# A transformer block on one core: W1, W2 and Wo copied inside DRAM into blocks with long runs, and loaded from the copies

## The chip, the core and the metric

The kernel runs on one core of a Trainium2 chip. Five engines work side by side, each through its own list of instructions: PE (matrix products; PEld is its weight load), ACT (exponentials and other functions), DVE (elementwise work), POOL (small work here) and SP, which here only issues DMAs. Semaphores tie them together. Sixteen DMA engines move data between DRAM and the on-chip memory SBUF, which has 128 partitions. Matrix products end in PSUM, eight banks of 128 x 512 fp32 values.

The metric is the device time of one execution in microseconds (us). The kernel before takes 1090.35 us (median of 3 runs, 1087.95 to 1093.55).

## What is computed

One pre-norm transformer layer on 2048 rows of width 1024, bf16, with 32 heads of width 32 and a feed-forward part of width 3584. `b1` and `b2` are the biases of the feed-forward part; `B_x` is not used.

```python
x = A_x
h = x + softmax_attention(layernorm(x) @ wqkv) @ wo      # 32 heads, no mask
h2 = h + gelu_tanh(layernorm(h) @ w1 + b1) @ w2 + b2
```

## The kernel before

**How the order comes about.** The program does not write its instruction lists by hand. `Graph.add` records tasks (a matmul group, an exponential, a DMA) with an estimated duration and the buffers that they read and write; `Graph.schedule` (L109) then simulates the engines with these estimates and fixes the order of every engine's list. `assign` gives each task the semaphore waits that the order does not already imply. For a DMA the planner charges an issue time, bytes divided by one fixed rate, and one fixed latency; it does not look at the length of a run. DMAs are issued by SP alone, in the planned order, over 24 "lanes" (semaphores); a DMA that has to wait holds up all that stand behind it on SP.

**Phases.** The 2048 rows are handled in eight units of 256 rows (`u` or `qb` = 0 to 7), and heads in eight groups `g` of four.

- Lead-in: x is loaded and normalized, transposed (`xnT`), and Q, K and V of group 0 are projected; the first exponentials start.
- First phase: for each further group, K and V are projected for all rows and Q for the rows needed soon, while attention runs for the row blocks 0 and 1 (and 2 for groups 1 and 2, `EXTRA`). In this phase the SBUF that later holds the feed-forward weights still holds `wqkv` (the tiles `Wall`) and `xnT`.
- Then come `late_q` (the Q of the remaining row blocks, from the normalized x that was parked in DRAM as `x_scratch`, loaded into `xq`), and for each unit `wo(u)` (output projection and first residual), `ln2(u)`, `ffn1(u)` (W1, bias, GELU) and `ffn2(u, j)` (W2 in two halves of 512 columns), all as background work beside the attention of later row blocks.
- The tail: after the last exponential, `wo`, `ffn1` and `ffn2` of unit 7 (and the second half of `ffn2` of unit 6) run alone.

**Attention round.** Each round issues eight score matmuls (L784), two exponentials of 128 x 1024 (L795), eight matmuls with V (L821) and a sum of the exponentials by pairs on DVE (L836) that is added up by matmuls with ones (L850). ACT is given score matmuls first (`pick_pe`): they have priority over all other work of PE. Background products go out either as one full 128-column matmul (L549, and L552 where they are planned so from the start) or as four narrow ones of 32 columns (L546), depending on what stands beside them.

**Weights.** W1 (1024 x 3584), W2 (3584 x 1024) and Wo (1024 x 1024) are read anew for every unit. `wblock` loads 256 columns of W1, Wo or `wqkv` into one of four ring slots `R.w1` (trace name a_w1r), 512 KB: partition p gets eight rows of 512 bytes. `ffn2` loads 512 rows x 512 columns of W2 into one of seven slots `R.w2` (a_w2r), 512 KB: four rows of 1 KB per partition. `wo` takes all four slots of `R.w1`, two for each half of the output columns. The tail has a second set of rings (b_w1r with 14 slots, b_w2r with 7) in the memory that K and V leave free. In the trace the inputs w1 and w2 both appear as in_B_w_dram.

Of the kernel before, what the change touches and what calls it, by code (L numbers as in the profile page):

```python
# [12 lines left out]
P = 128  # L13
BF = dt.bfloat16
# [314 lines left out]
def build_kernel(nc, A_x, A_wqkv, A_wo, B_w1, B_b1, B_w2, B_b2, out):  # L329
    _, S, D = A_x.shape  # L330
# [6 lines left out]
    DC = D // P  # L337
    FC = F // P
# [8 lines left out]
    gr = Graph(N_LANES)  # L347
# [18 lines left out]
    def sb(area, name, shape, dtype, split=1, parts=1):  # L366


        off, n = area.take(shape, dtype)
        h = nc.alloc_sbuf_tensor_at(name, shape, dtype, offset=off)  # L370
        step = n // split
        bufs = []
        for i in range(split):
            ps = [gr.buf("SB", off + i * step, off + (i + 1) * step, (name, i)) for _ in range(parts)]
            bufs.append(ps if parts > 1 else ps[0])
        return h, (bufs if split > 1 else bufs[0])
# [33 lines left out]
    OT, B_OT_ = sb(top, "OT", [P, 3, G, 256], BF, 3 * G, 2)  # L410
# [12 lines left out]
    for k in range(6):  # L423
        h, b = sb(k_hi if k == 2 else ph0, "Wall%d" % k, [P, DC, 512], BF, 1, 4)
# [57 lines left out]
            return i  # L482

    R1 = Rings((ffn, 4), (ffn, 7), ffn, 2)
    lq, B_lq = sb(xq_lo, "lq", [P, 2, 512], BF, 2)
    assert xq_lo.cur <= hn_lo
    att_area = Area(att_lo)
# [11 lines left out]
    qd = nc.dram_tensor("q_scratch", [G, NCH, P, 512], BF, kind="Internal").ap()  # L499
    xd = nc.dram_tensor("x_scratch", [3, P, DC, 512], BF, kind="Internal").ap()  # L500
    B_xd = [gr.buf() for _ in range(3)]
    B_qd = [[gr.buf() for _ in range(NCH)] for _ in range(G)]


# [13 lines left out]
    def slot(nrel=1):  # L518
        return Slot(gr.buf(), nrel, (6, 7))
# [374 lines left out]
            job.pv(r, s)  # L894


    def wblock(R, src_ap, prio=1):
        s = R.next("w1", R.nw1)
        dma(R.w1[:, s, :, :], src_ap.rearrange("(dc p) c -> p dc c", p=P), P * DC * 512, writes=[R.B_w1[s]], prio=prio)
        return s  # L900

    def wo(u, tail=False):
        R = R1
        nb = 0
        R.cnt["w1"] += -R.cnt["w1"] % 4
        ws = [wblock(R, A_wo[:, 256 * k:256 * k + 256]) for k in range(4)]
        assert ws == [0, 1, 2, 3]
        for t in range(2):
            hs = 2 * (u % 2) + t
            tt = 2 * u + t  # L910
            dma(hch[:, hs, :], x2[tt * P:(tt + 1) * P, :], P * 2048, writes=B_hch[hs], prio=1)
            for j in range(2):
                s = ws[2 * j]
                c = slice(512 * j, 512 * j + 512)
                bank = nb if tail else slot()
                nb += 1
                order = range(G) if tail else [7, 0, 1, 2, 3, 4, 5, 6]
                for k, g in enumerate(order):
                    mm(bank, OT[:, u % 3, g, t * P:(t + 1) * P], R.w1[:, s:s + 2, g, :], k == 0, k == 7 and not tail,
                       [B_OT[u % 3][g][t], R.B_w1[s], R.B_w1[s + 1]], not tail)  # L920
                if tail:
                    mm(bank, ident[:, :], hch[:, hs, c], False, True, [B_ident, B_hch[hs][j]], False)
                    act(lambda a, hs=hs, c=c, bank=bank: a.activation(hch[:, hs, c], psum[:, bank, :], ACT.Copy), 512,
                        reads=[bb(bank)], writes=[B_hch[hs][j]], prio=-1)
                else:
                    drop(dve(lambda v, hs=hs, c=c, bank=bank: v.tensor_tensor(
                        hch[:, hs, c], psum[:, bi(bank), :], hch[:, hs, c], ALU.add),
                        c_dve_ps(512), reads=[bb(bank), B_hch[hs][j]], writes=[B_hch[hs][j]]), bank)
# [14 lines left out]
    def ffn1(u, tail=False):  # L943
        R = R2 if tail else R1
        for blk in range(FC // 2):
            s = wblock(R, B_w1[:, 256 * blk:256 * blk + 256])
            bank = blk % 6 if tail else slot()
            for f in range(2):
                for dc in range(DC):
                    mm(bank, R.w1[:, s, dc, f * P:(f + 1) * P], hnT[:, dc, :], dc == 0, dc == DC - 1,  # L950
                       [R.B_w1[s]] + B_hnT, not tail, (256 * f, 256 * f + 256))
            evict1(u, 2 * blk, bank, tail)
            if not tail and blk % 2:
                gelu(u, blk // 2)
# [32 lines left out]
    def ffn2(u, j, wide=False, W=None, banks=None):  # L987
# [3 lines left out]
        ws = []  # L991
        for q in range(FC // 4):
            s = W.next("w2", W.nw2)
            dma(W.w2[:, s, :, :], B_w2[512 * q:512 * q + 512, c].rearrange("(f p) c -> p f c", p=P),
                P * 4096, writes=[W.B_w2[s]], prio=1)
            ws.append(s)
        for t in range(2):
            bank = banks[t] if banks and banks[t] is not None else slot()
# [113 lines left out]
        attention_drain()  # L1112

    EXTRA = [1, 2]
    for g in range(1, G):
        rest_of_projections(g)
        if g == 2:
            proj(0, 0, 1, slot(), "dve")
        attention(0, [g])
        attention(1, [g])  # L1120
        if g in EXTRA:
            attention(2, [g])
    for g in range(1, 2):
        if g not in EXTRA:
            proj(0, g, 1, slot(), "dve")
    late_q(1, 1, [g for g in range(2, G) if g not in EXTRA])
    wo(0)
    ln2(0)
# [149 lines left out]
```

## Time and profile before

| | |
|---|---|
| median of 3 runs | 1090.35 us |
| the profiled execution | 1091.97 us, of which its span (first to last instruction) 1090.2 us |
| busy: PE, ACT, DVE | 96%, 93%, 69% of the span |
| idle of ACT from 76 to 1021 us | 8.4 us |
| last exponential ends | about 1021.9 us |
| DMA packets | 280146, of which 274976 under 2 KB; 178.03 MB |
| W1 loads (98 and, for the tail, 14) | 512 KB each, median 4.4 and 6.1 us from issue to landing |
| W2 loads (105 and 7) | 512 KB each, 5.7 and 6.6 us |
| Wo loads (32) | 512 KB each, 4.2 us |

How to read the views that follow. The *page* gives busy time and a strip of 40 equal slices of the span, each digit the busy share in tenths. A row of the *windows* view is `from:to length, PE busy (x instructions) PEld ... POOL busy, granted clock of PE, DMA share, GB/s`; the DMA share is the mean busy share of 16 DMA engines, and since it is put together from packets it can come out a little over 1. A row of the *timeline* is `start, length, engine, line, operation, out<-in, count [idle before <- what ended it]`. A row of *groups* ends in `xcount: shortest/median/longest ns, first and last start in us`. "issue" as a releaser means that the engine waited for nothing that the profile shows. SPq is SP's queue, where the length of a row is the issue of the DMA alone, not its transfer.

### The profile page before, as it was taken

What the parts mean: (1) busy time and instruction counts of PE and PEld (TensorE: products, weight loads), DVE (VectorE), ACT (ScalarE), POOL (GpSimd) and SP (SyncE); (2) the same over time, 40 slices, a digit from 0 to 9 for tenths busy, and PEclk for the clock granted to TensorE, in tenths of its full rate; (3) what the DMA queues carried; (4) which work ended last, traced back from release to release, by engine and by line L of the source; (5) the groups of instructions that cost most, each with busy time, mean ns of one, the idle gap of its engine ahead of it and who ended that gap; (6) DMA issues with size and microseconds to landing.
All of it is one profiled execution on the core that took longest, in us unless ns stands there. A gap on an engine that the chain in (4) does not pass through costs nothing.

```text
span 1090.2 us, 41817 instructions
## 1 busy us (share of the span) xinstructions
PE 1045.6 (96%) x19048; PEld 609.6 (56%) x19107; DVE 755.9 (69%) x1453; ACT 1014.5 (93%) x1116; POOL 43.4 (4%) x110
## 2 busy tenths in 40 slices
PE   8989999998899999999999999999999999999998
PEld 6656555554344664574475457446545754474483
DVE  7886666666576896599489659948974967696401
ACT  4989999999999999999999999999999999999650
POOL 3200000000010001001000100100010000000100
PEclk9999999999999999999999999999999999899999
DMA  7640010008464667665685766567586656987370
GB/s 194 199 123 11 14 41 3 2 3 287 142 167 133 183 180 209 210 189 154 209 251 157 220 215 189 155 217 233 142 239 205 182 179 160 308 236 228 96 246 20
DMA packets 280146, 178.03 MB, mean 163 GB/s; under 512 B 42656, under 2 KB 274976, under 8 KB 279200
## 3 DMA queue, kind: packets, MB, share of 16 engines
q1 hardware_dynamic: 279968, 175.35, 54.1%
q8 instruction: 150, 2.46, 0.9%
q14 instruction: 28, 0.23, 0.1%
HBM read 161.16 MB, written 10.49 MB: 157 GB/s over the span
## 4 chain that ended last, share of the span: by engine, by line
PE 54%; ACT 39%; DVE 5%; issue 1%; DMA 1%; SPq 0%; POOL 0%; POOLq 0%; DVEq 0%
ACT PT L795 35%; PE ps L549 18%; PE ps L546 12%; PE ps L784 8%; PE ps L821 6%; PE ps L552 5%; PE ps L850 3%; ACT PX L795 2%; DVE PS L836 2%; ACT uu L983 2%; DMA xrb<-in_A_x_dram 0%; DVE OD L866 0%; PE ps L1025 0%; SPq L570 0%; DVE OD L873 0%
## 5 line engine op out<-in xcount | busy, mean ns | idle before, releaser
L795 ACT ACTIVATE PT<-ps 128x1024 bf16<-128x1024 f32 x992 | 922.4, 1082 | 14.7 <-PE ps L784 14.3
L836 DVE TENSOR_TENSOR PS<-PT 128x1024 bf16<-128x1024 bf16 x434 | 286.6, 685 | 128.9 <-PE ps L850 68.1
L784 PE MATMUL ps<-QT,KT 32*128 32x256 bf16 x4096 | 205.3, 274 | 10.7 <-ACT PT L795 5.4
L821 PE MATMUL ps<-PT,V 128*32 128x256 bf16 x3968 | 174.4, 274 | 2.8 <-ACT PT L795 2.8
L784 PEld LDWEIGHTS ps<-QT,KT 32*128 32x128 bf16 x4096 | 61.2, 92 | 166.3 <-ACT PT L795 134.8
L850 PE MATMUL ps<-PS,ones 128*32 128x256 bf16 x1792 | 124.6, 275 | 4.8 <-DVE PS L836 4.0
L821 PEld LDWEIGHTS ps<-PT,V 128*32 128x32 bf16 x3968 | 102.1, 97 | 29.4 <-issue 6.8
L549 PE MATMUL ps<-hnT,a_w1r 128*128 128x256 bf16 x949 | 116.5, 274 | 1.1 <-DVE gT L961 0.5
L549 PEld LDWEIGHTS ps<-hnT,a_w1r 128*128 128x128 bf16 x949 | 87.9, 98 | 25.8 <-issue 14.5
L546 PE MATMUL ps<-a_w2r,gT 128*32 128x512 bf16 x1372 | 98.3, 381 | 0.4 <-DVE hch L1007 0.2
L549 PE MATMUL ps<-a_w2r,gT 128*128 128x512 bf16 x382 | 93.8, 380 | 4.2 <-issue 2.9
L546 PE MATMUL ps<-hnT,a_w1r 128*32 128x256 bf16 x2476 | 88.9, 274 | 4.0 <-issue 1.6
L961 DVE TENSOR_TENSOR gT<-ps,b1f 128x512 bf16<-128x512 f32 x98 | 67.2, 686 | 17.5 <-PE ps L546 9.3
L546 PEld LDWEIGHTS ps<-hnT,a_w1r 128*32 128x32 bf16 x2476 | 60.4, 96 | 20.6 <-issue 16.8
L1007 DVE SCALAR_TENSOR_TENSOR hch<-ps,hch 128x512 bf16<-128x512 f32 x32 | 21.9, 685 | 69.9 <-PE ps L552 47.1
L850 PEld LDWEIGHTS ps<-PS,ones 128*32 128x32 bf16 x1792 | 47.0, 96 | 30.7 <-DVE PS L836 14.2
L549 PEld LDWEIGHTS ps<-a_w2r,gT 128*128 128x128 bf16 x413 | 35.2, 98 | 47.4 <-issue 13.4
L549 PE MATMUL ps<-xnT,Wall 128*128 128x512 bf16 (+1 forms) x256 | 53.5, 344 | 4.5 <-DVE rr L876 2.8
L983 ACT ACTIVATE uu<-uu 128x1024 bf16<-128x1024 bf16 x49 | 53.9, 1108 | 0.0
L546 PEld LDWEIGHTS ps<-a_w2r,gT 128*32 128x32 bf16 x1372 | 30.0, 96 | 25.6 <-issue 14.0
L603 POOL CAST mvb<-mv 128x2 bf16<-128x2 f32 (+1 forms) x25 | 4.9, 201 | 987.2 <-DVE mv L600 987.2
L549 PE MATMUL ps<-Wall,xnT 128*128 128x128 bf16 (+1 forms) x443 | 43.9, 247 | 0.0
(89 smaller groups left out, 1007.9 us busy)
## 6 DMA issues: line engine op xcount, KB each, us to landing
a_w2r<-in_B_w_dram SPq DMA_DIRECT2D x105, 512.0 KB, 5.7
a_w1r<-in_B_w_dram SPq DMA_DIRECT2D x98, 512.0 KB, 4.4
a_w1r<-in_A_wo_dram SPq DMA_DIRECT2D x32, 512.0 KB, 4.2
b_w1r<-in_B_w_dram SPq DMA_DIRECT2D x14, 512.0 KB, 6.1
a_w1r<-in_A_wqkv_dram SPq DMA_DIRECT2D x11, 512.0 KB, 5.0
Wall<-in_A_wqkv_dram SPq DMA_DIRECT2D x17, 256.0 KB, 4.7
xrb<-in_A_x_dram SPq DMA_DIRECT2D x16, 256.0 KB, 4.0
hch<-in_A_x_dram SPq DMA_DIRECT2D x16, 256.0 KB, 5.2
```

The costliest lines, as they stand in the source:

```text
L546: fns.append(lambda p, j=j: p.matmul(psum[32 * j:32 * j + 32, bi(bank), c0:c1], lhsT[:, 32 * j:32 * j + 32], rhs, start=start, stop=stop, ...
L549: t.whole = lambda p: p.matmul(psum[:, bi(bank), c0:c1], lhsT, rhs, start=start, stop=stop, skip_group_check=True)
L552: t = pe(lambda p: p.matmul(psum[:, bi(bank), c0:c1], lhsT, rhs, start=start, stop=stop), occ, reads=reads, writes=[bb(bank)], mode="full" ...
L603: pool(lambda g: g.tensor_copy(mvb[:, sl, :], mv_l[:, sl, :]), 0.25, reads=B_mv[sl], writes=B_mvb[sl], prio=prio)
L784: return p.matmul(psum[:, 2 * us[h // 2] + h % 2, 256 * i:256 * i + 256], KT[32 * h:32 * h + 32, g, k0:k0 + P], QT[32 * h:32 * h + 32, qs, :],
L795: act(lambda a, u=u, k=k: a.activation(PTs[s][:, k, :, :], psum[:, 2 * u:2 * u + 2, :], ACT.Exp, bias=0.0, scale=SCALE), 1024, reads=[B_ps ...
L821: fns.append(lambda p, i=i, h=h: p.matmul(psum[32 * h:32 * h + 32, bi(bank), 0:256], V[:, g, 2 * r + i, 32 * h:32 * h + 32], PTs[s][:, h / ...
L836: dve(lambda v: v.tensor_tensor(PS[:, n, :, :], pairs[:, :, 0:256], pairs[:, :, 256:512], ALU.add), c_dve(1024, 2), reads=B_PTs[s], writes ...
L850: fns.append(lambda p, h=h, rhs=rhs, i=i: p.matmul(psum[32 * h:32 * h + 32, bi(bank), 256:512], ones32[:, :], rhs, start=False, stop=last, ...
L961: t = dve(lambda v: v.tensor_tensor(g[:, fc:fc + 2, :], psum[:, bi(bank), :].rearrange("p (f c) -> p f c", f=2), b1f[:, fc:fc + 2].unsquee ...
L983: act(lambda a: a.activation(w, w, ACT.Tanh, bias=0.0, scale=KT2), 1024, reads=[B_uu[i]], writes=[B_uu[i]], prio=-1)
L1007: drop(dve(lambda v, hs=hs, bank=bank, half=half: v.scalar_tensor_tensor(hch[:, hs, c], psum[:, bi(bank), :], half, hch[:, hs, c], ALU.mul ...
```

## The change

At the end of the first phase's recording, `block_copies` adds 30 DMAs from DRAM to DRAM: Wo in two blocks of 512 columns (1 MB each), W1 in 14 blocks of 256 columns and W2 in 14 blocks of 512 rows x 512 columns (512 KB each). Each block is laid out as SBUF wants it, so that a partition's part is one run: 8 KB for Wo, 4 KB for W1 and W2. The copies read their source in the same rows of 512 bytes or 1 KB as the loads did. Copy number i waits for exponential number `COPY0 + COPY_STEP * i` (96, 101, ... 241, counted from 0), has priority 3 and is issued by SP like every other DMA. All later loads of W1, W2 and Wo, the tail's too, read the copies and depend on them. Loads of `wqkv` for `late_q` stay as they were.

Wo is now loaded in two DMAs of 1 MB in place of four of 512 KB; the tiles `wov` lie over slots 0, 1 and 2, 3 of the ring `R.w1`, and the products of `wo` read them there. All products and sizes stay the same, and so do the planner's costs.

```diff
@@ -482,6 +482,7 @@
     R1 = Rings((ffn, 4), (ffn, 7), ffn, 2)
+    wov = [nc.alloc_sbuf_tensor_at("wov%d" % j, [P, DC, 512], BF, offset=R1.B_w1[2 * j].lo) for j in range(2)]
@@ -499,6 +500,12 @@
     B_xd = [gr.buf() for _ in range(3)]
+    w1d = nc.dram_tensor("w1_blocks", [FC // 2, P, DC, 256], BF, kind="Internal").ap()
+    w2d = nc.dram_tensor("w2_blocks", [2, FC // 4, P, 4, 512], BF, kind="Internal").ap()
+    wod = nc.dram_tensor("wo_blocks", [2, P, DC, 512], BF, kind="Internal").ap()
+    B_w1d = [gr.buf() for _ in range(FC // 2)]
+    B_w2d = [[gr.buf() for _ in range(FC // 4)] for _ in range(2)]
+    B_wod = [gr.buf() for _ in range(2)]
@@ -894,8 +901,26 @@
-    def wblock(R, src_ap, prio=1):
+    def block_copies():
+
+        jobs = []
+        for j in range(2):
+            jobs.append((wod[j], A_wo[:, 512 * j:512 * j + 512].rearrange("(dc p) c -> p dc c", p=P), P * DC * 1024, B_wod[j]))
+        for k in range(FC // 2):
+            jobs.append((w1d[k], B_w1[:, 256 * k:256 * k + 256].rearrange("(dc p) c -> p dc c", p=P), P * DC * 512, B_w1d[k]))
+        for j in range(2):
+            for q in range(FC // 4):
+                jobs.append((w2d[j, q], B_w2[512 * q:512 * q + 512, 512 * j:512 * j + 512].rearrange("(f p) c -> p f c", p=P),
+                             P * 4096, B_w2d[j][q]))
+        exps = [t for t in gr.tasks if t.kind == "exp"]
+        for i, (o_ap, i_ap, n, b) in enumerate(jobs):
+            dma(o_ap, i_ap, n, writes=[b], prio=3, after=[exps[COPY0 + COPY_STEP * i]])
+
+    def wblock(R, src_ap, prio=1, block=None):
         s = R.next("w1", R.nw1)
+        if block is not None:
+            dma(R.w1[:, s, :, :], w1d[block], P * DC * 512, reads=[B_w1d[block]], writes=[R.B_w1[s]], prio=prio)
+            return s
         dma(R.w1[:, s, :, :], src_ap.rearrange("(dc p) c -> p dc c", p=P), P * DC * 512, writes=[R.B_w1[s]], prio=prio)
         return s
@@ -903,20 +928,21 @@
         R.cnt["w1"] += -R.cnt["w1"] % 4
-        ws = [wblock(R, A_wo[:, 256 * k:256 * k + 256]) for k in range(4)]
-        assert ws == [0, 1, 2, 3]
+        for j in range(2):
+            dma(wov[j][:, :, :], wod[j], P * DC * 1024, reads=[B_wod[j]], writes=R.B_w1[2 * j:2 * j + 2], prio=1)
+        R.cnt["w1"] += 4
...
-                s = ws[2 * j]
+                s = 2 * j
...
-                    mm(bank, OT[:, u % 3, g, t * P:(t + 1) * P], R.w1[:, s:s + 2, g, :], k == 0, k == 7 and not tail,
+                    mm(bank, OT[:, u % 3, g, t * P:(t + 1) * P], wov[j][:, g, :], k == 0, k == 7 and not tail,
@@ -943,7 +969,7 @@
-            s = wblock(R, B_w1[:, 256 * blk:256 * blk + 256])
+            s = wblock(R, None, block=blk)
@@ -991,8 +1017,7 @@
-            dma(W.w2[:, s, :, :], B_w2[512 * q:512 * q + 512, c].rearrange("(f p) c -> p f c", p=P),
-                P * 4096, writes=[W.B_w2[s]], prio=1)
+            dma(W.w2[:, s, :, :], w2d[j, q], P * 4096, reads=[B_w2d[j][q]], writes=[W.B_w2[s]], prio=1)
@@ -1112,6 +1137,7 @@
     EXTRA = [1, 2]
+    COPY0, COPY_STEP = 96, 5
@@ -1123,6 +1149,7 @@
+    block_copies()
     late_q(1, 1, [g for g in range(2, G) if g not in EXTRA])
```

## The prediction

> **What bounds the kernel now.** I read the page's parts on busy time, slices and the chain first, then busy time by stage, then the tiles that the change loads.
>
> ```profile
> span 1090.2 us, 41817 instructions
> PE 1045.6 (96%) x19048; PEld 609.6 (56%) x19107; DVE 755.9 (69%) x1453; ACT 1014.5 (93%) x1116; POOL 43.4 (4%) x110
> DMA  7640010008464667665685766567586656987370
> ...
> q1 hardware_dynamic: 279968, 175.35, 54.1%
> PE 54%; ACT 39%; DVE 5%; issue 1%; DMA 1%; SPq 0%; POOL 0%; POOLq 0%; DVEq 0%
> ```
>
> ```profile
> core 0: us, PE busy (x) PEld busy (x) DVE busy (x) ACT busy (x) POOL busy (x), PEclk, DMA share, GB/s
> 76.00:273.00 197.00, 191.45 (x3941) 113.25 (x3952) 122.55 (x223) 196.26 (x214) 0.00 (x0) 1.00 0.18 57
> 273.00:293.00 20.00, 18.22 (x257) 7.66 (x256) 9.99 (x19) 18.34 (x20) 0.00 (x0) 0.92 0.42 128
> 293.00:1021.00 728.00, 704.63 (x13435) 403.56 (x13470) 547.12 (x1050) 721.97 (x785) 22.23 (x56) 0.99 0.67 196
> 1021.00:1090.00 69.00, 65.51 (x431) 40.03 (x434) 10.76 (x22) 20.23 (x37) 3.45 (x8) 0.98 0.38 124
> ```
>
> From 76 to 1021 us ACT never stops for long: it is idle 197 - 196.26 = 0.7 us, then 1.7 us, then 728 - 721.97 = 6.0 us, 8.4 us in all. Behind 1021 us only PE matters, 65.5 of 69 us busy. So the end is set by ACT's row of exponentials and then by a tail of matmuls; the chain gives DMA 1%. The queues are loaded (0.67 of the 16 engines), but what counts is whether somebody waits for a load:
>
> ```profile
> its engine sat idle before it (us, times) until:
>   issue: 30.3, 146
> ...
>   DMA QT<-q_scratch: 0.2, 1
> ```
>
> That is the view of the W2 ring's tile a_w2r. Its matmuls sat idle 0.2 us for any transfer at all, and for a small Q block; the same view of a_w1r (W1 and Wo) lists no DMA. In this trace all loads of the three weights are hidden. That leaves a change of these loads no more than the 8.4 us above, and of it only what DMA causes.
>
> **Part 1, the loads in long runs.** Rates come from stages in which one packet size prevails (512 B for W1, 1 KB for W2, 8 KB for the Q input xq), as GB/s over DMA share:
>
> ```profile
> 370.00:390.00 20.00, 19.64 (x413) 14.56 (x406) 19.63 (x39) 20.00 (x23) 0.00 (x0) 1.00 0.63 183
> 515.00:532.00 17.00, 16.62 (x280) 7.66 (x275) 10.04 (x21) 17.00 (x19) 0.00 (x0) 1.00 0.84 257
> 262.00:266.00 4.00, 3.22 (x69) 1.39 (x70) 3.23 (x9) 4.00 (x5) 0.00 (x0) 1.00 1.02 431
> ```
>
> 183/0.63 = 290, 257/0.84 = 306 and 431/1.02 = 423 GB/s. A block of 524 KB takes the queue 1.81, 1.71 or 1.24 us. For 4 KB I take 400, near the upper row: 1.31 us. So some 0.45 us are saved on each of 224 loads of W1 and W2 and 1.1 us on each pair of Wo, about 120 us of queue time, all of it at places where nobody waits: 0 on the end, unless DMA load slows something else. There is one trace of that:
>
> ```profile
> 431.00:434.00 3.00, 2.04 (x45) 0.80 (x37) 2.73 (x7) 2.18 (x3) 0.00 (x0) 1.00 1.09 375
> 814.00:817.00 3.00, 1.83 (x51) 1.00 (x43) 2.56 (x7) 2.27 (x3) 0.00 (x0) 1.00 1.07 360
> ```
>
> ```profile
> 434.31 0.28 PE L784 MATMUL ps<-QT,KT 32*128 32x256 bf16 x3 [1.23 <-issue]
> 817.32 0.39 PE L784 MATMUL ps<-QT,KT 32*128 32x256 bf16 x5 [1.49 <-issue]
> ```
>
> ```profile
> 434.64 28.72 ACT L795 ACTIVATE PT<-ps 128x1024 bf16<-128x1024 f32 x31 [1.46 <-PE ps L784]
> 817.74 28.83 ACT L795 ACTIVATE PT<-ps 128x1024 bf16<-128x1024 f32 x31 [1.47 <-PE ps L784]
> ```
>
> Both times PE stops inside a group of eight score matmuls, where the program has no wait ("issue": it waited for nothing that the profile shows), at the end of a burst of W2 loads with the DMA engines full. I read it as PE's instructions arriving late behind the loads. ACT loses 1.46 + 1.47 = 2.9 us. A burst that is a quarter shorter may save all or nothing of this; I take half: -1.5 us.
>
> A rule of the Trainium skill speaks for more. "Perfetto Trace Analysis", section DMA Optimizations, says that transfers under 2 KB carry much overhead and that going to 4 or 8 KB can raise throughput dramatically. The rates above agree in direction (290 to 423 GB/s), but the page ties it to kernels that are DMA-bound, which this one is not.
>
> **Part 2, the copies.** 30 copies are added on SP's queue (2 of Wo with 1 MB, 14 each of W1 and W2 with 524 KB), 16 Wo loads fall away. Each copy waits for an exponential, the 97th and then every fifth:
>
> ```profile
> 65.06 7.65 ACT L795 ACTIVATE PT<-ps 128x1024 bf16<-128x1024 f32 x8
> 76.51 197.17 ACT L795 ACTIVATE PT<-ps 128x1024 bf16<-128x1024 f32 x214 [3.80 <-PE ps L784]
> ```
>
> ```profile
> 125.50 0.32 SPq L570 DMA_DIRECT2D QT<-q_scratch  x1
> ...
> 142.37 0.38 SPq L570 DMA_DIRECT2D a_w1r<-in_A_wqkv_dram  x1
> 250.01 1.48 SPq L570 DMA_DIRECT2D a_w2r<-in_B_w_dram  x3
> ...
> 258.24 3.41 SPq L570 DMA_DIRECT2D xq<-x_scratch  x2
> 264.89 0.38 SPq L570 DMA_DIRECT2D a_w1r<-in_A_wqkv_dram  x1
> ```
>
> ```profile
> 113.00:253.00 140.00, 138.35 (x2734) 80.64 (x2739) 89.03 (x163) 140.00 (x153) 0.00 (x0) 1.00 0.06 16
> ```
>
> 197.17/214 = 0.92 us each. 56 exponentials lie ahead of 76.5 us (48 of the lead-in's 24 rounds, and the 8 of the first row), so the first copy is released at 76.5 + 41 x 0.92 = 114 us and the last at 76.5 + 186 x 0.92 = 248 us, one per 4.6 us. There the DMA share is 0.06 and SP sits from 142 to 250 us in one wait, so the issues (0.38 us each) cost nothing. Behind a copy's wait stand only a few small Q transfers until 142 us; the built order keeps each between the copies that frame it. The Q block loaded at 125.5 us comes while about the 110th exponential runs; it belongs to the ninth pair of row block and group (16 exponentials each), which begins with the 129th, some 19 x 0.92 = 17 us later. One copy ahead of it in the queue does not use that up.
>
> No row shows a DRAM to DRAM transfer. Lower bound: the price of a load with the same packets, 1.81 us (W1) and 1.71 us (W2). Upper: reading and then writing, twice that, 3.6 us. Both fit in 4.6 us. I take the upper one for the queue's share: 2 x 6.8 + 14 x 3.6 + 14 x 3.4 = 112 us in 134 us, 0.84 against 0.06; at the lower it is 0.42. What that load does to PE's instructions I price by the later stage, 6.0 us of ACT idle in 728 us at 0.67: 134/728 x 6.0 x (0.42 to 0.84)/0.67 = 0.7 to 1.4 us, from 0 if it has nothing to do with load. I take +0.7.
>
> The last copy is released 2 us ahead of the burst at 250 us. What is late then is the second xq load, the first that PE waits for after it:
>
> ```profile
> L546 PEld LDWEIGHTS ps<-xq,a_w1r x212: 92/97/97, 272.7 to 351.0; 128*32 128x32 bf16 x106
> ...
> DMA to landing us min/median/max: 5.0/7.0/7.4
> ```
>
> It is issued at about 261.3 and lands 7.0 us later, at 268.3; PE reads it from 272.7. The slack of 4.4 us covers a copy's 3.6 us, and the burst ahead of it has shrunk by one Wo load and three shorter W2 loads. Cost 0; if that cover were gone, PE stands at this matmul in its fixed order, the scores behind it come late, and ACT idles for the whole lateness.
>
> **Part 3, Wo in two pieces of 1 MB.** Each needs two ring slots free where a 512 KB load needed one.
>
> ```profile
> a_w1r<-in_A_wo_dram SPq DMA_DIRECT2D x32, 512.0 KB, 4.2
> ...
> x_scratch<-xnT SPq DMA_DIRECT2D x1, 1024.0 KB, 3.8
> ```
>
> The second row is the only 1 MB transfer in 8 KB packets that ran alone (a store, window 40 to 80 us): 3.8 us. A Wo piece in one run lands as early as half of it did: 0, between -0.4 and +0.65 us (2.48 us at 423 GB/s against 1.81).
>
> **Part 4, the order.** The planner is greedy and charges bytes, not packets, so it takes no profit from longer runs. In the built program PE, ACT, DVE and POOL run the same work as before in the same order up to the first xq matmuls; behind it background groups move by a few places, and a net 23 more of them go out as four narrow matmuls. What that can cost shows where PE had too little to do:
>
> ```profile
> 265.00:270.00 5.00, 3.07 (x72) 1.35 (x72) 2.60 (x5) 5.00 (x7) 0.00 (x0) 1.00 0.98 337
> 270.00:275.00 5.00, 3.47 (x46) 1.25 (x48) 2.08 (x3) 4.81 (x7) 0.00 (x0) 0.79 0.62 214
> ```
>
> After 5 us at 61% busy the granted clock falls (0.79), and ACT loses the 1.7 us of 273 to 293 us. One such place more or fewer is -1.7 to +1.7 us; the built order leaves fewer background groups beside the scores ahead of the first Wo stage, so I take half a place to the bad side, +0.8.
>
> **Sum.** -1.5 + 0.7 + 0 + 0.8 = 0.0 us. The profiled run took 1091.97 us, 1.8 us beyond its span, and lies 1.6 us above the median of 1090.35 (1087.95 to 1093.55). Unchanged, the forecast is **1090.4 us**. With all bounds, -2.9 - 1.7 to +1.4 + 1.7, the likeliest case's own range is 1085.8 to 1093.5.
>
> **Rivals.** *A, the copies do not keep up (slower).* From 4.6 + 4.4/28 = 4.8 us per copy on, the backlog at 248 us eats the slack and falls on xq. At three times a load's price, 5.3 us: 28 x 0.7 - 4.4 = 15 us, 1105 us; at 5.0 us, 1097. For it: nothing here shows such a transfer, and its source rows jump by 128 rows. Against: the loads from the same rows reach 290 GB/s, and it takes 2.7 times their price. Chance 0.13.
> The Trainium skill has a rule for it: "DMA: Bandwidth & Descriptors", section Latency and other measured facts, gives copies between HBM tensors 207 GB/s at a row pitch of 512 KiB and 103 GB/s at 4 MiB. By the page's two figures a copy of 524 KB would take 2.5 or 5.1 us, an estimate; the second would make rival A true, and no run here shows it yet.
>
> *B, the order costs (slower).* Six Wo stages with loads 0.65 us later, 3.9 us, and one thin place more, 1.7 us: 1096 us, if PE has no other group ready. Against: Wo now lands in 3.8 us where it landed in 4.2. Chance 0.12.
>
> *C, the queue was the cause of ACT's idle time (faster).* Then with a fifth less load (120 of the queue's 0.54 x 1090 = 590 us) most of the 8.4 us goes, say 6 us: 1084.4. For it: both large gaps lie in full queues, and 113 to 253 us has no ACT idle at a share of 0.06. Against: many full stretches have no gap. The Trace Analysis rule above would speak for it. Chance 0.15.
>
> **Chances.** Forecast 0.60, A 0.13, B 0.12, C 0.15. Taking 0.5% (5.5 us, about what a measurement of this kernel can tell from no change): faster 0.15, within 0.60, slower 0.25. The range 1084.5 to 1099 holds the likeliest case, C's edge, B, and A's near end.
>
> **What would show it.** Right: copies landing within 4.6 us of issue, DMA share between 0.4 and 0.85 from 114 to 248 us, no idle of PE for xq at 272 us; DMA share in W1 stages down by a quarter; ACT idle between 293 and 1021 us within 2 us of 6.0. Wrong: PE idle at the first xq matmul (A), idle or clock dips at the Wo stages (B), ACT idle below 3 us (C), or an idle place that none of the steps names.

## The result and the profile after

| | before | after |
|---|---|---|
| median, 22 runs of each | 1092.95 us (1086.62 to 1096.41) | 1087.16 us (1085.63 to 1092.03) |
| ratio of the times | | 0.9958, 95% interval [0.9947, 0.9969] |
| the profiled execution, its span | 1091.97, 1090.2 us | 1086.23, 1084.4 us |
| last exponential ends (this execution) | 1021.87 us | 1017.91 us |

The change makes the kernel faster by 0.4%. That is less than the 0.5% that the prediction took as the bound of what counts as faster, but the interval leaves out 1, and the prediction had put the sum of all its steps at 0.0 us. A second set of 12 runs (below) gave 0.9966 [0.9953, 0.998]. The median of the kernel before over these 22 runs lies 2.6 us above the 1090.35 us of three runs from which the forecast started. So the time of 1087.16 us is only 3.2 us below the forecast of 1090.4 us, by the luck of that start; the change itself is -4.8 us by the means and -5.8 us by the medians.

The page of the kernel after, the same parts as were shown of before:

```profile
span 1084.4 us, 41995 instructions
PE 1042.4 (96%) x19119; PEld 610.4 (56%) x19176; DVE 759.3 (70%) x1453; ACT 1013.3 (93%) x1116; POOL 43.2 (4%) x110
DMA  7640444438564546654664664476466465876260
...
q1 hardware_dynamic: 129664, 192.12, 53.2%
ACT 64%; PE 29%; DVE 4%; issue 1%; POOL 1%; DMA 0%; SPq 0%; POOLq 0%; DVEq 0%
```

The packets fall from 279968 to 129664 although 17 MB more are moved; the strip shows the copies as the digits 4, 4, 4, 4, 3 where before had 0, 1, 0, 0, 0. The chain changes from PE 54%, ACT 39% to ACT 64%, PE 29%, which fits a row of exponentials that is interrupted less often.

The same stages in windows of the kernel after:

```profile
core 0: us, PE busy (x) PEld busy (x) DVE busy (x) ACT busy (x) POOL busy (x), PEclk, DMA share, GB/s
114.00:248.00 134.00, 132.40 (x2674) 77.87 (x2675) 84.29 (x154) 134.00 (x147) 0.00 (x0) 1.00 0.43 134
273.00:277.00 4.00, 3.49 (x55) 1.61 (x59) 1.29 (x2) 4.00 (x5) 0.00 (x0) 1.00 0.18 60
293.00:297.00 4.00, 3.53 (x22) 1.14 (x23) 1.70 (x3) 2.83 (x4) 0.00 (x0) 0.57 0.29 94
265.00:315.00 50.00, 42.98 (x664) 18.76 (x670) 31.73 (x62) 48.47 (x53) 3.12 (x7) 0.97 0.64 194
315.00:1016.00 701.00, 681.39 (x13195) 394.89 (x13223) 532.25 (x1013) 697.89 (x760) 18.94 (x50) 1.00 0.58 198
370.00:390.00 20.00, 19.92 (x361) 14.94 (x357) 19.04 (x38) 20.00 (x23) 0.00 (x0) 1.00 0.49 167
515.00:532.00 17.00, 16.24 (x295) 7.51 (x293) 7.89 (x14) 16.26 (x19) 0.00 (x0) 1.00 0.68 245
```

And four of them of the kernel before, for the comparison (the long stage is cut at 1016 us, where both kernels still run exponentials):

```profile
273.00:277.00 4.00, 3.67 (x33) 1.17 (x34) 0.69 (x1) 2.78 (x4) 0.00 (x0) 0.59 0.09 26
293.00:297.00 4.00, 2.21 (x23) 0.84 (x23) 2.93 (x7) 4.00 (x6) 0.00 (x0) 1.00 0.93 297
265.00:315.00 50.00, 42.88 (x672) 18.47 (x677) 31.83 (x62) 48.30 (x53) 3.09 (x8) 0.97 0.65 186
315.00:1016.00 701.00, 681.10 (x13048) 393.08 (x13080) 526.62 (x1011) 695.00 (x755) 19.15 (x48) 1.00 0.67 198
```

ACT's idle time (the length of the window less ACT's busy time) is what sets the end. From 265 to 315 us it goes from 1.70 to 1.53 us only; from 315 to 1016 us it falls from 6.00 to 3.11 us. Together that is 3.06 us, of the 3.96 us by which the last exponential ends earlier in these two executions. The remaining 1.8 us of the difference between the two spans lies behind the last exponential (1090.2 - 1021.87 = 68.3 us against 1084.4 - 1017.91 = 66.5 us); there both kernels do the same work, and 68.3 to 69.1 us or 66.5 us turn up with old and new versions alike, so it is not counted for the change.

The thin stretch of PE that the prediction named shows in the timeline of PE. Before:

```profile
270.79 0.29 PE L850 MATMUL ps<-PS,ones 128*32 128x256 bf16 x4 [0.32 <-DVE PS L836]
271.02 0.40 PE L784 MATMUL ps<-QT,KT 32*128 32x256 bf16 x8
...
272.75 0.53 PE L546 MATMUL ps<-xq,a_w1r 128*32 128x512 bf16 x4
273.21 0.61 PE L784 MATMUL ps<-QT,KT 32*128 32x256 bf16 x8
274.15 2.30 PE L549 MATMUL ps<-xq,a_w1r 128*128 128x512 bf16 x5 [0.33 <-issue]
```

The same place after (the lines of the file have moved by 7), and what follows 20 us later:

```profile
270.85 0.29 PE L857 MATMUL ps<-PS,ones 128*32 128x256 bf16 x4 [0.32 <-DVE PS L843]
270.97 0.39 PE L553 MATMUL ps<-xq,a_w1r 128*32 128x512 bf16 x4
271.29 0.40 PE L791 MATMUL ps<-QT,KT 32*128 32x256 bf16 x8
271.84 1.24 PE L556 MATMUL ps<-xq,a_w1r 128*128 128x512 bf16 x5 [0.16 <-issue]
...
294.08 2.68 PE L556 MATMUL ps<-wov,OT 128*128 128x512 bf16 x6 [0.33 <-issue]
296.69 0.40 PE L791 MATMUL ps<-QT,KT 32*128 32x256 bf16 x8
297.02 1.47 PE L556 MATMUL ps<-wov,OT 128*128 128x512 bf16 x6
```

ACT's timeline of the kernel before and, in the second fence, of the kernel after:

```profile
276.83 15.01 ACT L795 ACTIVATE PT<-ps 128x1024 bf16<-128x1024 f32 x16 [1.03 <-PE ps L784]
292.27 28.73 ACT L795 ACTIVATE PT<-ps 128x1024 bf16<-128x1024 f32 x31 [0.43 <-PE ps L784]
```

```profile
261.67 34.16 ACT L802 ACTIVATE PT<-ps 128x1024 bf16<-128x1024 f32 x37
297.14 11.12 ACT L802 ACTIVATE PT<-ps 128x1024 bf16<-128x1024 f32 x12 [1.31 <-PE ps L791]
```

The new order has the first xq products one round of scores earlier, at 270.97 in place of 272.75 us. Before, the granted clock falls behind this thin stretch (0.59 from 273 to 277 us); five xq matmuls then take 2.30 us where they take 1.24 us after, the scores behind them come late, and ACT loses 1.7 us up to 293 us. After, the clock stays at 1.00 there, but it falls at the first Wo stage instead (0.57 from 293 to 297 us): six Wo matmuls take 2.68 us and the next six 1.47 us, and ACT loses 1.31 us at 297 us, where the kernel before loses nothing. So in these two executions the loss has moved by 20 us and has not gone. A window that ends at 293 us counts the move as a gain; the gain lies behind 315 us.

### The profile page after: what moved, and what is told of

Same layout as the page of the kernel before. It is cut to its first block, busy times and chain, and to the rows that moved or that the text cites. A ratio compares the mean times of both kernels' runs of the same rounds, so it can differ in the third digit from the quotient of the medians.

```text
span 1084.4 us, 41995 instructions
## 1 busy us (share of the span) xinstructions
PE 1042.4 (96%) x19119; PEld 610.4 (56%) x19176; DVE 759.3 (70%) x1453; ACT 1013.3 (93%) x1116; POOL 43.2 (4%) x110
## 3 DMA queue, kind: packets, MB, share of 16 engines
q1 hardware_dynamic: 129664, 192.12, 53.2%
## 4 chain that ended last, share of the span: by engine, by line
ACT 64%; PE 29%; DVE 4%; issue 1%; POOL 1%; DMA 0%; SPq 0%; POOLq 0%; DVEq 0%
ACT PT L802 59%; PE ps L556 9%; PE ps L553 6%; PE ps L559 5%; PE ps L791 4%; ACT uu L1009 3%; PE ps L828 3%; ACT PX L802 2%; PE ps L857 1%; DVE PS L843 1%; DVE st L605 1%; DMA xrb<-in_A_x_dram 0%; DVE hch L952 0%; POOL denb L614 0%; DVE uu L1008 0%
## 5 line engine op out<-in xcount | busy, mean ns | idle before, releaser
L556 PE MATMUL ps<-hnT,a_w1r 128*128 128x256 bf16 x979 | 119.1, 273 | 2.0 <-DVE hch L1032 1.2
L556 PEld LDWEIGHTS ps<-hnT,a_w1r 128*128 128x128 bf16 x979 | 90.1, 98 | 27.1 <-issue 16.1
L556 PE MATMUL ps<-a_w2r,gT 128*128 128x512 bf16 x390 | 96.2, 380 | 2.8 <-issue 1.9
L553 PE MATMUL ps<-hnT,a_w1r 128*32 128x256 bf16 x2356 | 82.9, 275 | 1.5 <-DVE gT L987 0.9
```

Of the source, the lines that this page charges most:

```text
L553: fns.append(lambda p, j=j: p.matmul(psum[32 * j:32 * j + 32, bi(bank), c0:c1], lhsT[:, 32 * j:32 * j + 32], rhs, start=start, stop=stop, ...
L556: t.whole = lambda p: p.matmul(psum[:, bi(bank), c0:c1], lhsT, rhs, start=start, stop=stop, skip_group_check=True)
```

## The experiments

The changed kernel differs in four things: it adds copies, it loads in long runs, it loads Wo in two pieces, and its instructions stand in another order. The order follows from the two Wo pieces alone: a kernel before with nothing changed but these has, on PE, ACT, DVE and POOL, exactly the order of the kernel after. So order, copies and long runs can be combined freely. In the tables "old" and "new" name these two orders. Where Wo is loaded from its source in two pieces, its rows are of 1 KB instead of 512 B; in the tables that still counts as short. Ratios are to the kernel before, in runs of the same job on the same chip.

### Order, copies and run length apart

`order_only`, against the kernel before:

```diff
-        ws = [wblock(R, A_wo[:, 256 * k:256 * k + 256]) for k in range(4)]
-        assert ws == [0, 1, 2, 3]
+        for j in range(2):
+            dma(wov[j][:, :, :], A_wo[:, 512 * j:512 * j + 512].rearrange("(dc p) c -> p dc c", p=P), P * DC * 1024, writes=R.B_w1[2 * j:2 * j + 2], prio=1)
+        R.cnt["w1"] += 4
...
```

> The kernel before with one edit: Wo is loaded from its source in two DMAs of 1 MB (rows of 1 KB) instead of four of 512 KB. No copies, W1 and W2 read in short runs. PE, ACT, DVE and POOL then have exactly the order of the changed kernel. Theory order (the moved background groups bring the gain): ratio to before 0.996, ACT idle between 76 us and the last exponential down by 3 us as in the changed kernel. Theory runs (long runs bring it, by freeing PE's supply of instructions): 1.000, idle as before.

`long_runs_old_order`: all copies and long runs, Wo in four pieces, and so the old order; against the kernel after:

```diff
-        for j in range(2):
-            jobs.append((wod[j], A_wo[:, 512 * j:512 * j + 512].rearrange("(dc p) c -> p dc c", p=P), P * DC * 1024, B_wod[j]))
+        for j in range(4):
+            jobs.append((wod[j], A_wo[:, 256 * j:256 * j + 256].rearrange("(dc p) c -> p dc c", p=P), P * DC * 512, B_wod[j]))
...
+        ws = [wblock(R, None, src=(wod[k], B_wod[k])) for k in range(4)]
...
-    COPY0, COPY_STEP = 96, 5
+    COPY0, COPY_STEP = 86, 5
```

> The kernel before with copies and long runs for W1, W2 and Wo, but Wo still in four loads of 512 KB (4 KB runs), 32 copies. PE, ACT, DVE and POOL keep exactly the order of the kernel before. Theory order: 1.000. Theory runs: 0.996, and the stops of PE of over 0.45 us inside a group without a wait, 7 before, fall to 2 or 3.

`copies_alone`: the kernel before with the 30 copies, which nothing reads:

```diff
+    COPY0, COPY_STEP = 96, 5
...
+    block_copies()
```

> The kernel before with the 30 copies added, which nothing reads; all loads as before, order of the engines as before. Both theories: 1.000 to 1.001; ACT idle from 113 to 253 us 0 to 1.4 us, copies landing about 4 us after issue. Above 1.002 the copies have a price that the changed kernel earns back elsewhere.

`copies_short_runs`: the kernel after, its loads read the sources again (and still wait for the copies):

```diff
-            dma(R.w1[:, s, :, :], w1d[block], P * DC * 512, reads=[B_w1d[block]], writes=[R.B_w1[s]], prio=prio)
+            dma(R.w1[:, s, :, :], B_w1[:, 256 * block:256 * block + 256].rearrange("(dc p) c -> p dc c", p=P), P * DC * 512, reads=[B_w1d[block]], writes=[R.B_w1[s]], prio=prio)
...
```

> The changed kernel, copies included, with all loads reading W1, W2 and Wo from the sources in short runs again. Order of the engines as in the changed kernel. Theory order: 0.996, like the changed kernel. Theory runs: 1.000.

Measured, 12 runs of each (the kernel before: 35 runs, mean 1091.3 us). The idle times are ACT's in one profiled execution. "Stops" are the places between 76 and 1016 us where PE's timeline shows over 0.3 us of idle time that end in "issue", with their sum. Left out are eleven rows of 0.33 us in all traces together: each stands ahead of a full product in a stretch with the granted clock halved, as at 274.15 and 294.08 us above. The expectations count differently: gaps in which neither a product nor a weight load runs, by what the weight load waits for. That gives 6.5 us at 10 places in the kernel before; at four of the ten the product behind the weight load waits for DVE, so they are not counted here.

| kernel | order, runs, copies | mean us | ratio [95%] | ACT idle 265-315 / 315-1016 | stops |
|---|---|---|---|---|---|
| before | old, short, none | 1091.3 | 1 | 1.70 / 6.00 | 4.70 us, 6 |
| copies_alone | old, short, 30 | 1092.2 | 1.0012 [0.9996, 1.0029] | 2.60 / 6.14 | 5.15 us, 6 |
| long_runs_old_order | old, long, 32 | 1089.3 | 0.9986 [0.9971, 1.0] | 4.14 / 3.44 | 1.85 us, 3 |
| order_only | new, short, none | 1088.8 | 0.9975 [0.995, 1.0] | 1.49 / 2.89 | 0.37 us, 1 |
| copies_short_runs | new, short, 30 | 1089.5 | 0.9984 [0.9966, 1.0002] | 1.67 / 4.29 | 2.53 us, 5 |
| after (its own 22 runs; before there: 1092.4) | new, long, 30 | 1087.6 | 0.9958 [0.9947, 0.9969] | 1.53 / 3.11 | 2.06 us, 3 |

Windows behind the table, of copies_alone, long_runs_old_order and order_only in this order:

```profile
315.00:1016.00 701.00, 679.70 (x13009) 392.43 (x13041) 527.62 (x1012) 694.86 (x755) 19.17 (x48) 1.00 0.67 198
```

```profile
315.00:1016.00 701.00, 683.62 (x13058) 394.11 (x13095) 528.73 (x1018) 697.56 (x758) 19.63 (x49) 1.00 0.59 199
```

```profile
315.00:1016.00 701.00, 682.67 (x13201) 395.24 (x13229) 531.90 (x1012) 698.11 (x759) 18.41 (x48) 1.00 0.65 198
```

From the means: the copies cost +0.9 us (old order, standard error 0.8, so a cost is not shown); the order, with copies and short runs on both sides, brings 1089.5 - 1092.25 = -2.75 us (1.0); the long runs, with copies and the old order on both sides, bring 1089.3 - 1092.25 = -2.96 us (0.9). The sum is -4.8 us (1.2); the whole change measured -4.8 (0.6) and, in the second set, -3.7 (0.6). So two parts bring the gain, neither of them all of it, and neither of the two theories of the expectations, order alone or runs alone, holds.

ACT's idle time from 315 to 1016 us points the same way: 6.0 and 6.1 us with the old order and short runs, 3.4 us with long runs, 2.9 and 4.3 us with the new order and short runs, 3.1 us with both. These are single executions: order_only and copies_short_runs have the same order and loads there and differ by 1.4 us, and so the idle times cannot tell whether the two gains add up or overlap. At 265 to 315 us the new order loses 1.5 to 1.7 us in this table and the old one 1.7, 2.6 and 4.1 us, as the clock falls there once or twice in an execution.

### How much the loads can cost at all

`tiny_old_order` and `tiny_new_order`: after the first fill of the rings the loads bring 16 of the 128 partitions, so that the products use stale weights in the others. Against the kernel before (the second one has Wo in two pieces as well, from other rows of Wo):

```diff
...
+            n = P if W.cnt["w2"] <= W.nw2 else 16
-            dma(W.w2[:, s, :, :], B_w2[512 * q:512 * q + 512, c].rearrange("(f p) c -> p f c", p=P),
+            dma(W.w2[0:n, s, :, :], B_w2[512 * q:512 * q + 512, c].rearrange("(f p) c -> p f c", p=P)[0:n],
...
```

> The kernel before, with every load of W1, W2 and Wo in the ring after its first filling cut to 16 of 128 partitions (an eighth of the bytes and packets; the rest of a slot keeps an older block, so the output is not the reference's; the tail's second rings are loaded whole). Order of the engines as before. DMA share from 293 to 1016 us should fall from 0.67 to about 0.2. If DMA load slows PE (theory runs): PE's stops without a wait vanish and the ratio to before is 0.995 or less. If DMA load costs nothing (theory order): 1.000.

> The same cut with the order of the changed kernel: Wo in two loads (from arbitrary rows of Wo, 16 partitions after the first unit), no copies; the output is not the reference's. Theory order: faster than the run with the old order by 2.5 to 3 us, since the order's gain does not hang on DMA. Theory runs: equal to it within 1 us, since the order only moved PE's dense stretches away from full queues.

`more_load_old_order`: the kernel before with 90 copies that nothing reads, one after every seventh exponential from the 331st on:

```diff
+            for k in range(3):
+                dma(o_ap, i_ap, 0, writes=[b], prio=3, after=[exps[COPY0 + COPY_STEP * (30 * k + i)]])
...
+    COPY0, COPY_STEP = 330, 7
```

> The kernel before with 90 copies of 0.5 to 1 MB between DRAM and DRAM, which nothing reads, one per seven exponentials from the 331st on; order of the engines as before. DMA share from 293 to 1016 us from 0.67 to about 0.95. Theory runs: PE's stops without a wait rise from some 5 us to 8 or more and the ratio to before is 1.003 or more. Theory order: 1.000 to 1.001.

| kernel | runs | ratio [95%] | ACT idle 265-315 / 315-1016 | stops |
|---|---|---|---|---|
| tiny_old_order | 7 | 0.9955 [0.9938, 0.9972] | 3.58 / 0.82 | none |
| tiny_new_order | 12 | 0.996 [0.9945, 0.9974] | 2.15 / 3.12 | 2.23 us, 2 |
| more_load_old_order | 6 | 1.0217 [1.0191, 1.0243] | 2.22 / 27.79 | 15.95 us, 16 |

Windows of tiny_old_order and, in the second fence, of more_load_old_order:

```profile
315.00:1016.00 701.00, 690.02 (x13171) 394.90 (x13169) 530.26 (x1017) 700.18 (x762) 19.15 (x48) 1.00 0.25 66
```

```profile
315.00:1016.00 701.00, 669.23 (x12644) 383.89 (x12640) 514.97 (x986) 673.21 (x728) 19.14 (x48) 0.99 0.87 262
```

With the same instructions in the same order, ACT's idle time in this stage goes from 0.8 us at a DMA share of 0.25 over 6.0 us at 0.67 to 27.8 us at 0.87: the loads cost time although PE waits for hardly any of them, and steeply more as the queues fill. In the kernel with more load the groups of PE that lost most (columns: busy and mean, then idle time ahead and what ended it) say how:

```profile
L790 PE MATMUL ps<-QT,KT 32*128 32x256 bf16 x4096 | 206.7, 275 | 11.7 <-ACT PT L801 5.6 <-issue 4.8 <-ACT PX L801 0.7
...
L552 PE MATMUL ps<-hnT,a_w1r 128*32 128x256 bf16 x2476 | 90.7, 276 | 14.0 <-issue 9.9 <-DMA a_w1r<-in_B_w_dram 1.8 <-DVE OD L879 1.5
```

"issue" ends 4.8 and 9.9 us of their idle time, late W1 loads 1.8 us: most of it is PE standing without a wait. With nearly all loads gone and the old order the ratio is 0.9955. So the weight traffic costs the kernel before some 5 us, of which the long runs alone recover 2 to 3.

In this pair the new order brings nothing: by the means it is 1.3 us slower (0.9), where the theory that its gain does not hang on the loads expected 2.5 to 3 us faster. It loses less at 265 to 315 us and more behind, 2.23 us of it at two stops at 370 and 389 us, in the rings' first fill, which is still with full loads. So the order's gain of 2.75 us was found only with the full loads.

### Why PE stands: its instructions

`narrow_groups`: the order and loads of the kernel before; every background product goes out as four narrow matmuls. In the function that merges the planned tiles:

```diff
-            if k == 0 or sum(x.occ for x in run[k:]) >= 3.0:
+            if False:
```

> The kernel before, its order and loads kept, with every background product that goes out as one full matmul issued as four narrow ones: 2281 matmuls become 9124, 6843 more matmuls and as many more weight loads, DMA data the same. A group of four is busy some 0.006 us longer than a full one, 14 us over the span. Theory S (the supply of PE's instructions): PE's stops of over 0.3 us without a wait, 6.5 us in the kernel before, go to 12 us or more, most of them at the ends of W2 bursts where the kernel before has them; time 1103 to 1125 us. Rival (the stops are contention for something else, such as SBUF or the data queues themselves, which PE's instruction count does not change): stops stay at 5 to 8 us; time 1092 to 1106 us.

It took 1128.44 us (one run). The page of narrow_groups:

```profile
span 1126.7 us, 55881 instructions
PE 1067.3 (95%) x26107; PEld 629.7 (56%) x26112; DVE 758.0 (67%) x1453; ACT 1020.7 (91%) x1116; POOL 43.5 (4%) x110
...
q8 instruction: 204, 3.34, 1.2%
```

Before, the last of these lines reads:

```profile
q8 instruction: 150, 2.46, 0.9%
```

The instructions themselves come over a DMA queue: 14064 instructions more are 54 packets of 16.4 KB more, some 260 for each. The stops grew from 4.70 us at 6 places to 25.14 us at 30 (counted here to 1060 us, since the stage ends later), with the same loads. The timeline of PE from 84 us on shows where they fall:

```profile
84.62 0.84 PE L546 MATMUL ps<-Wall,xnT 128*32 128x128 bf16 x45 [1.28 <-issue]
85.39 0.40 PE L784 MATMUL ps<-QT,KT 32*128 32x256 bf16 x8
85.72 1.24 PE L546 MATMUL ps<-Wall,xnT 128*32 128x128 bf16 x75
88.34 0.56 PE L546 MATMUL ps<-Wall,xnT 128*32 128x128 bf16 x25 [1.38 <-issue]
88.84 0.40 PE L784 MATMUL ps<-QT,KT 32*128 32x256 bf16 x8
89.17 1.52 PE L546 MATMUL ps<-Wall,xnT 128*32 128x128 bf16 x95
91.80 0.34 PE L546 MATMUL ps<-Wall,xnT 128*32 128x128 bf16 x9 [1.11 <-issue]
```

From one stop to the next there are 45 + 8 + 75 = 128 and 25 + 8 + 95 = 128 products, each with its weight load: 256 instructions both times. That is one packet (150 packets of 256 are 38400; on PE the kernel before has 19107 weight loads, as many products and 180 other instructions, 38394 in all). The 14 packed traces settle it. They hold 85 stops, and at every one of them PE had started 256 instructions for each packet landed so far and 193 or 194 more; it went on 1.2 to 1.65 us after the last of these packets had ended. Where these 193 come from the traces do not tell; but the number is the same at every stop, while at PE's other gaps of over 0.3 us its place in a packet takes all kinds of values. So PE stands there because it has used up its instructions.

More data with the same instructions and more instructions with the same data both lengthen these stops. Of the 36 us by which narrow_groups is longer, PE's busy time, 1067.3 - 1045.6 = 21.7 us more, is the other part; the two together are more than 36 us, so not all of either lengthens the run. The expected 1103 to 1125 us, made with 14 us for the busy time, were too low, and the rival's 5 to 8 us of stops is far off. Five of the 30 stops lie from 84 to 100 us, where no W2 is loaded, so they do not all stand at the ends of W2 bursts, as was expected of most.

### Which loads, and the change again

`w2_only_long` (against the kernel after; only W2's 14 copies stay) and `w1_wo_long` (only the 16 of W1 and Wo):

```diff
-            dma(R.w1[:, s, :, :], w1d[block], P * DC * 512, reads=[B_w1d[block]], writes=[R.B_w1[s]], prio=prio)
+            dma(R.w1[:, s, :, :], B_w1[:, 256 * block:256 * block + 256].rearrange("(dc p) c -> p dc c", p=P), P * DC * 512, writes=[R.B_w1[s]], prio=prio)
...
-    COPY0, COPY_STEP = 96, 5
+    COPY0, COPY_STEP = 96, 10
```

```diff
-            dma(W.w2[:, s, :, :], w2d[j, q], P * 4096, reads=[B_w2d[j][q]], writes=[W.B_w2[s]], prio=1)
+            dma(W.w2[:, s, :, :], B_w2[512 * q:512 * q + 512, c].rearrange("(f p) c -> p f c", p=P), P * 4096, writes=[W.B_w2[s]], prio=1)
...
-    COPY0, COPY_STEP = 96, 5
+    COPY0, COPY_STEP = 96, 9
```

> The new order; only W2 is copied (14 copies, one after every tenth exponential) and loaded in 4 KB runs, W1 and Wo come from the sources in 512 B runs, Wo in two loads. Theory S (PE's instructions come late behind full data queues; runs of W2 loads are what fills them): the W2 loads carry most of the gain of the long runs, and 16 copies fewer give 0.4 us back: ratio 0.9955 to 0.9970 to the kernel before, PE's stops of over 0.3 us without a wait 2 to 3.5 us in all. Rival O (the order alone counts, run length nothing): 0.9975 to 0.998, as the new order without copies. Rival W1 (it is the 512 B packets that count, whatever comes in bursts): 0.9975 to 0.999, since these stay.

> The new order; W1 and Wo are copied (16 copies, one after every ninth exponential) and loaded in runs of 4 and 8 KB, W2 comes from the source in 1 KB runs. Theory S: the W2 bursts stay as long as before, so little of the long runs' gain is left: 0.997 to 0.9985, stops without a wait 3 to 5 us in all. Rival O: the same ratio as the kernel with W2 alone, 0.9975 to 0.998. Rival W1: 0.9955 to 0.997, stops 2 to 3 us.

`changed_again` is the kernel after, unedited.

> The changed kernel again, for the comparison inside this job. Theory S and rival O both: 0.9958 as recorded, 0.994 to 0.9975, with a new profiled execution; stops without a wait 2 to 3.5 us. It is the measure for the two kernels with some of the copies: if W2 alone reaches its ratio, 16 of the 30 copies are worth nothing.

| kernel, 12 runs each | ratio [95%] | ACT idle 265-315 / 315-1016 | stops |
|---|---|---|---|
| w2_only_long | 0.9974 [0.9959, 0.999] | 2.32 / 4.41 | 1.35 us, 3 |
| w1_wo_long | 0.9975 [0.996, 0.9989] | 2.12 / 4.46 | 2.24 us, 4 |
| changed_again | 0.9966 [0.9953, 0.998] | 1.51 / 2.40 | 0.53 us, 1 |

The two halves are alike, and like the order alone (0.9975). That W2's bursts carry the gain of the long runs is not borne out: the time of w2_only_long was expected at 0.9955 to 0.9970. That run length counts for nothing (both at 0.9975, the whole also) is not excluded by this job alone, since the whole is only 0.8 us below the halves with a standard error of 0.7 us. With half of the run-length gain for each half (-2.75 + 0.45 - 1.5 = -3.8 us), 0.9965 was to be expected, which lies in both intervals. Neither half is faster than the whole.

Windows of changed_again, the same program as after in another execution:

```profile
265.00:315.00 50.00, 42.77 (x670) 18.64 (x677) 32.20 (x62) 48.49 (x54) 2.53 (x6) 0.97 0.62 196
315.00:1016.00 701.00, 683.50 (x13198) 395.51 (x13226) 532.70 (x1013) 698.60 (x760) 19.58 (x51) 0.99 0.57 198
```

It loses 1.51 us at 265 to 315 us, as the first execution does. The stops are not at the same places: the largest was at 653 us (1.18 us) in the first execution, and the only one here is at 734 us (0.53 us). Their sums, 2.06 and 0.53 us, differ by 1.5 us for one and the same program. So a single stop is chance, and so is a difference of one or two us between the sums of single executions; that none are left with the loads gone and 16 and 25 us come with more load or more instructions is not.

### A plan that knows of the long runs

`long_runs_cheaper_plan`: the kernel after, with the planner charging 0.7 of the bytes for loads from the copies, which gives a third order:

```diff
-            dma(W.w2[:, s, :, :], w2d[j, q], P * 4096, reads=[B_w2d[j][q]], writes=[W.B_w2[s]], prio=1)
+            dma(W.w2[:, s, :, :], w2d[j, q], int(P * 4096 * 0.7), reads=[B_w2d[j][q]], writes=[W.B_w2[s]], prio=1)
...
```

> The changed kernel with the planner's bytes of the loads from the copies taken times 0.7, about what they take (280/0.7 = 400 GB/s). Same work, another order after 269 us. If the order that came with the change was a lucky one, this one lies between it and the kernel before (ratio 0.996 to 0.999). If the planner's price matters in itself, it is faster than the changed kernel (0.995 or less).

Ratio 0.9977 [0.996, 0.9993] over 12 runs, stops 3.63 us at 5 places, ACT idle 1.77 and 6.19 us: no better than the kernel after, in the range that was expected if the order of the change was a lucky one. By the means it lies 0.5 and 1.6 us above the two sets of the kernel after, which is not clear of noise. No version that does the whole work is faster than the kernel after.

## Why the prediction failed, step by step

**What bounds the kernel: right.** The end is set by ACT's row of exponentials, and no more than its 8.4 us of idle time could be had. The change took about half of it, and the kernel with nearly no weight traffic no more than that.

**Part 1, the loads in long runs: mechanism right, size put low.** The prediction saw PE's two stops, read them as late instructions behind the loads, bounded their cost at 2.9 us and took half, -1.5 us. The runs show -2.96 us (standard error 0.9), the full bound; the half was a choice with no row behind it, but it lies only 1.7 standard errors off. Nor are the two large stops the whole of it: there are six, and they shrink in sum from 4.70 us (5.15 with the copies) to 1.85 us with the order kept. The rates, on the other hand, were taken too high: from the windows after, W1 runs at 167 / 0.49 = 341 and W2 at 245 / 0.68 = 360 GB/s where 400 was assumed, so a block takes 1.54 or 1.46 us and saves 0.27 or 0.25 us rather than 0.45. "Perfetto Trace Analysis" of the Trainium skill, section DMA Optimizations, says that longer transfers can raise throughput dramatically; here it is 290 to 341 and 306 to 360 GB/s, 18% in both cases, and worth 0.3% of the time.

**Part 2, the copies: they keep up, as predicted; their price is not shown.** They ran at the lower bound, not at the upper one that was taken for the share:

```profile
a_w2r<-w_blocks SPq DMA_DIRECT2D x105, 512.0 KB, 5.8
a_w1r<-w_blocks SPq DMA_DIRECT2D x98, 512.0 KB, 3.9
wov<-wo_blocks SPq DMA_DIRECT2D x16, 1024.0 KB, 4.8
w_blocks<-in_B_w_dram SPq DMA_DIRECT2D x28, 512.0 KB, 4.0
```

These are the DMA issues of the page after, the last column from issue to landing. A copy lands in 4.0 us where a load of the same block took 4.4 (W1) or 5.7 us (W2), and the share from 114 to 248 us is 0.43, the 0.42 of the lower bound. Before, it is 0.04 there, so (0.43 - 0.04) x 134 = 52 us for 32 blocks of 512 KB are 1.6 us each. "DMA: Bandwidth & Descriptors" of the Trainium skill, section Latency and other measured facts, states its two figures, which gave 2.5 or 5.1 us by estimate, for row pitches of 512 KiB and 4 MiB; the rows here lie 7 KB (W1) or 2 KB (W2, Wo) apart, and neither figure shows. Rival A, which needed the second, fell. PE found its xq in time: its first xq product moved ahead, from 272.75 to 270.97 us. The price of +0.7 us was to be idle time of ACT beside the copies, and there is none: ACT is busy 134.00 of 134 us from 114 to 248 us with the copies, as it was without them. That +0.9 us (0.8) was measured is therefore no proof of the term; nothing is also within its noise.

**Part 3, Wo in pieces of 1 MB: as bounded.** A piece lands in 4.8 us where half of it took 4.2, near the upper bound of +0.65 us, and rival B's late Wo stages did not come: the kernel with nothing but these pieces and their order has 0.9975 [0.995, 1.0], so it is not slower.

**Part 4, the order: this step failed, with the wrong sign and most of the effect left out.** The prediction priced the order by the thin stretch alone (265 to 275 us, clock 0.79, 1.7 us for one such place) and put half a place to the bad side, +0.8, from a count of background groups ahead of the first Wo stage. The runs show -2.75 us (1.0), and most of it not at such a place. The drop of the clock moved: with the old order the five executions other than narrow_groups have it at 271 to 273 us and two of them again at 295 to 296 us; with the new order all seven have it at 292 to 295 us and three of them also at 270 to 271 us. From 265 to 315 us these five lose 1.7 to 4.1 us (mean 2.8) and the seven 1.5 to 2.3 us (mean 1.8), so up to 1 us may lie there; between the kernels before and after it is 0.17 us. The larger part lies behind 315 us, where ACT's idle time with short runs falls from 6.0 and 6.1 us to 2.9 and 4.3 us and the stops from 4.70 and 5.15 us to 0.37 and 2.53 us. With the loads cut away the order brings nothing. So the order seems to work through the same stops as the long runs, by what PE has to do while the queues are full; the prediction let the queue act on the long runs only and had no term for this. Which of the moved groups do it was not tried.

**The sum.** With the measured terms in place of the assumed ones it reads -2.96 + 0.9 + 0 - 2.75 = -4.8 us in place of 0.0. Rival C (1084.4 us, chance 0.15) came nearest: the queue was indeed a cause of ACT's idle time. But it expected 6 us from a lighter queue alone, and the long runs gave half of that; and its sign, ACT idle below 3 us from 293 to 1021 us, did not come (723 - 718.36 = 4.64 and 723 - 719.31 = 3.69 us from 293 to 1016 us in the two executions). The prediction's own sign of being right, idle within 2 us of 6.0, holds in the first execution and just fails in the second: it is too wide, and single executions are too noisy, to tell a change of 4.8 us from none.

**Open.** No single part has an interval that excludes 1 by much; the split between order and run length is good to about 1 us. Whether W1 or W2 counts more is not settled, nor whether the two gains would stay as large one without the other, nor how the new order shortens the stops.

## What to carry to other kernels

A load that nobody waits for is not free: look for gaps of PE that end without a releaser, sum them over the whole trace, and price them by a kernel with the loads cut away and one with loads added before you price any edit of the loads. Where an edit moves a greedy planner's order, do not price the order from one thin stretch of the profile: a kernel in which only the order is changed measures it. And before a place of loss is called gone, look at the next 50 us: here it had moved by 20 us, just past the end of the window.

## What the runs showed of the hardware that was not expected

PE's instructions share the DMA engines with the data, in packets of 16.4 KB with 256 instructions each, and PE can run out of them. It does so with almost empty queues too, where the instructions are short enough. Window 84 to 100 us of narrow_groups, and then the 150 us behind it:

```profile
84.00:100.00 16.00, 11.46 (x529) 8.51 (x533) 5.84 (x10) 10.28 (x12) 0.00 (x0) 1.00 0.03 8
100.00:250.00 150.00, 149.62 (x3926) 89.12 (x3922) 95.21 (x176) 149.84 (x163) 0.00 (x0) 1.00 0.05 14
```

At a DMA share of 0.03, 529 + 533 instructions in 11.46 us of busy time, 93 per us, bring stops of 0.64 to 1.38 us (5 of them, 5.2 us) and cost ACT 5.7 of 16 us; at 52 per us, right behind, there is none. From stop to stop 3.5 to 4.0 us pass, for 256 instructions that PE works off in 2.8 us at 93 per us and in 4.9 us at 52 per us. Splitting a product into four narrow matmuls has this price besides its longer busy time.
